# Two stores on two queues, merged waits and an earlier bias product in the tail of an attention and Mish decode kernel

## The chip, the cores and the metric

The kernel runs on one core of a Trainium2 chip. The metric is the device time of one execution in microseconds (us), and lower is better. The kernel before takes 669.4 us. Within one job its executions spread over 0.5 to 0.7 us.

## The reference, cut to what matters

```python
def reference(A_x, A_k_cache, A_v_cache, A_wq, A_wo, B_x, B_w1, B_b1, B_w2):
    # attention over a cache: 4 sequences, 32 heads, 4096 positions, head size 128
    h = x + attention(layernorm(x), k_cache, v_cache, wq) @ wo       # 4 x 640
    # feed-forward: 640 -> 1728 -> 640, Mish activation
    g = layernorm(h) @ w1 + b1
    act = g * tanh(softplus(g))
    return h + act @ w2                                              # 4 x 640, bf16
```

The two caches, read once, are 268 MB; all weights together are under 15 MB. What the change touches comes after the last cache tile: output projection, second layer norm, feed-forward and the store of 4 x 640 numbers.

## The kernel before

Some words first. SBUF is the memory in which the engines' tiles lie; its rows are called partitions. An engine *issues* a DMA, a transfer between memories; the DMA has *landed* when the last update of its semaphore (a counter that engines wait on) is seen. Of the two operands of a matmul, the *stationary* one is loaded into the array of TensorE first (LDWEIGHTS in a trace), and the *moving* one then passes through it (MATMUL). The *cast* below turns the result into bf16 before it is stored.

The kernel is written engine by engine. A small class keeps the semaphores: `need` waits for named results and `do` issues an instruction that may announce one. TensorE's main loop is a hardware loop, so some semaphores are counted back down by whoever waits on them (they are "taken"). Such a wait is an instruction of its own:

```python
            if sem in self.take:
                self.log.append((sem, d))
                if self.live:
                    self.eng.wait_ge(h, d).then_inc(h, -d)   # a separate instruction
            elif self.live:
                self.eng.wait_ge(h, n)                       # can ride on the next instruction
```

The tail of TensorE's program, cut:

```python
        wo_mm(2)
        wo_mm(3)                                   # each waits for its piece of wo
        ...                                        # sums for the layer norm
        pe.need("cen")
        for c0, c1 in zip(W1S, W1S[1:]):           # two pieces of w1
            pe.need(("w1", c0))
            if c1 == DC:
                pe.need("b1s")
                mm(red[:, 2, 0 : FC * N], ident_f[:, :], b1s[...], False, False)   # bias product
            for j in [FM] + list(range(FM)):       # the odd 64 features first, then 13 x 128
                ...                                # w1 products
        pe.need("h_lo")
        ...                                        # h (two bf16 parts) added to the result
        pe.need("act")
        def w2_mm(j):
            rows = P if j < FM else FT             # 128, or 64 for the odd features
            for k in range(CG):                    # four column groups of 160 outputs
                mm(y2_ps[k * QD : k * QD + N, :], act[0:rows, j, :], w2_..., ...)
        pe.need("w2t")
        w2_mm(FM)
        for j0, j1 in zip(W2S, W2S[1:]):           # three pieces of w2
            pe.need(("w2", j0))
            ...
```

The four column groups of the array compute 160 of the 640 outputs each. The four result rows of group k land in partitions 32k to 32k+3, and SyncE stores each group by itself:

```python
        sp.need("o_bf")
        for q in range(CG):
            load(sp, out_rows[:, q * OC : (q + 1) * OC], o_bf[q * QD : q * QD + N, :], ("out", q), "OUT")
        sp.need(("out", CG - 1))
```

The softmax here doesn't subtract the row's maximum and nothing guards it: scores larger than these inputs give would overflow.

Of the kernel before, what the change touches and what calls it, by code (L numbers as in the profile page):

```python
# [8 lines left out]
BF16 = mybir.dt.bfloat16  # L9
ACT = mybir.ActivationFunctionType  # L10
ALU = mybir.AluOpType
# [3 lines left out]
class Prog:  # L15
# [7 lines left out]
    def restart(self, live):  # L23
        self.live = live
        self.seen = {}
        self.count = {}
        self.log = []

    def need(self, *keys):
        if not self.book.ready:  # L30
            return
        want = {}
        for k in keys:
            sem, n = self.book.marks[k]
            if n > self.seen.get(sem, 0):
                want[sem] = max(n, want.get(sem, 0))
        for sem, n in want.items():
            d = n - self.seen.get(sem, 0)
            self.seen[sem] = n
            h = self.book.handles[sem]  # L40
            if sem in self.take:
                self.log.append((sem, d))
                if self.live:
                    self.eng.wait_ge(h, d).then_inc(h, -d)  # L44
            elif self.live:
                self.eng.wait_ge(h, n)

    def do(self, fn, mark=None, sem=None, by=1):
        ins = fn() if self.live else None
# [17 lines left out]
def kernel(  # L67
# [15 lines left out]
    N, _, D = A_x.shape  # L83
    _, H, Sk, Dh = A_k_cache.shape
    F = B_w1.shape[1]
    P = 128
# [14 lines left out]
    CG = 4  # L101
# [9 lines left out]

    book = Book()
    WSEM = ["WQ", "WT"] + [f"W{k}" for k in range(9)]
    for s in ["PE", "DV", "DVP", "DVA", "AC", "ACP", "PO", "KA", "KB", "VA", "VC", "X", "S", "OUT"] + WSEM:
        book.handles[s] = tc.alloc_semaphore(s)

    SB0, SLOT0 = 16512, 229344 - 3 * SLOT * 2
# [2 lines left out]
    def sb(name, shape, dt, region=at, top=SLOT0):  # L120
        size = 4 if dt == FP32 else 2
        for d in shape[1:]:
            size *= d
        size = -(-size // 32) * 32
        t = nc.alloc_sbuf_tensor_at(name, shape, dt, offset=region[0]).ap()
        region[0] += size
        assert region[0] <= top, (name, region[0])
        return t
# [61 lines left out]
    std2 = sb("std2", (P, N), FP32, tail, topA)  # L190
    rstd = sb("rstd", (P, N), FP32, tail, topA)
    b1s = sb("b1s", (P, FC, N), FP32, tail, topA)
    h_hi = sb("h_hi", (P, DC, N), BF16, tail, topA)
    h_lo = sb("h_lo", (P, DC, N), BF16, tail, topA)
    h1 = sb("h1", (P, FC, N), FP32, tail, topA)
    ta = sb("ta", (P, FC, N), FP32, tail, topA)
    tb = sb("tb", (P, FC, N), FP32, tail, topA)
    tb2 = sb("tb2", (P, FC, N), FP32, tail, topA)
    tb3 = sb("tb3", (P, FC, N), FP32, tail, topA)
    hm2 = sb("hm2", (P, FC, N), FP32, tail, topA)  # L200
    act = sb("act", (P, FC, N), BF16, tail, topA)
    o_bf = sb("o_bf", (P, OC), BF16, tail, topA)

    red = nc.alloc_psum_tensor("red", (P, 4, 512), FP32).ap()
# [32 lines left out]

    def load(p, dst, src, key, sem):
        p.do(lambda: p.eng.dma_start(out=dst, in_=src), key, sem, 16)

    def sync_prog():
        load(sp, slot["C"][:, 0 : DC * H * Dh], A_wq.rearrange("(p c) n -> p (c n)", c=DC), "wq", "WQ")

        def k_load(i):
            s = KS[i % N]
            load(sp, slot[s][:, :], tiles(A_k_cache, i), ("K", i), "K" + s)

        def v_load(i):
            s = VS[i % N]
            load(sp, slot[s][:, :], tiles(A_v_cache, i), ("V", i), "V" + s)  # L250

        for hg in range(NHG):
            i = hg * N
            if hg:
                sp.need(("PV", i - 2))
            k_load(i)
            if hg:
                sp.need(("F", i - 1, NS - 1))
            k_load(i + 1)
            sp.need(("PV", i - 1) if hg else ("qb", NHG - 1))  # L260
            v_load(i)
            sp.need(("F", i, NS - 1))
            k_load(i + 2)
            sp.need(("PV", i))
            v_load(i + 1)
            sp.need(("F", i + 1, NS - 1))
            k_load(i + 3)
            sp.need(("F", i + 2, NS - 1))
            v_load(i + 2)
            sp.need(("PV", i + 1))  # L270
            v_load(i + 3)
        sp.need(("F", NT - 1, NS - 1))
        for q in range(NHG):
            load(
                sp, wo_sb[:, q, :, :],
                A_wo[q * QN : (q + 1) * QN, :].rearrange("(p j) n -> p j n", j=G), ("wo", q), f"W{q}",
            )
        w1_v = B_w1.rearrange("(p c) n -> p c n", c=DC)
        for k, (c0, c1) in enumerate(zip(W1S, W1S[1:])):
            load(sp, w1_sb[:, c0:c1, :], w1_v[:, c0:c1, :], ("w1", c0), f"W{NHG + k}")  # L280
        sp.need(("PV", NT - 2))
        load(sp, w2_tail[0:FT, :], B_w2[FM * P : F, :], "w2t", "WT")
        w2_v = B_w2[0 : FM * P, :].rearrange("(p j) n -> p j n", j=FM)
        for k, (j0, j1) in enumerate(zip(W2S, W2S[1:])):
            load(sp, w2_sb[:, j0:j1, :], w2_v[:, j0:j1, :], ("w2", j0), f"W{NHG + 2 + k}")
        sp.need("o_bf")
        for q in range(CG):
            load(
                sp, out_rows[:, q * OC : (q + 1) * OC], o_bf[q * QD : q * QD + N, :],
                ("out", q), "OUT",  # L290
            )
        sp.need(("out", CG - 1))

    def pool_prog():
        g = nc.gpsimd
        po.do(lambda: g.memset(ident[:, :], 0.0), "id0", "PO")
        po.need("id0")
        po.do(
            lambda: g.affine_select(
                out=ident[:, :], in_=ident[:, :], compare_op=ALU.not_equal, fill=1.0, base=0,  # L300
                pattern=[[-1, P]], channel_multiplier=1,
            ),
            "ident", "PO",
        )
        po.do(lambda: g.memset(b1T[:, :], 0.0), "b1z", "PO")
        po.do(lambda: g.memset(lnT[:, :, :], 0.0), "lnz", "PO")
        po.do(lambda: g.memset(sel[:, :, :], 0.0), "selz", "PO")
        po.do(lambda: g.memset(selo[:, :, :], 0.0), "seloz", "PO")
        po.do(lambda: g.memset(ones[:, :], 1.0), "ones", "PO")
        po.need(("PV", NT - 2))  # L310
        po.do(lambda: g.memset(ones_d[:, :], 1.0 / D), "ones_d", "PO")
        po.do(lambda: g.memset(zeros[:, :], 0.0), "zeros", "PO")
        po.do(lambda: g.tensor_copy(out=ident_f[:, :], in_=ident[:, :]), "ident_f", "PO")

    def act_prog():
# [48 lines left out]
        for i in range(NT):  # L364
# [17 lines left out]
            lambda: a.activation(out=ta[:, :, :], in_=h1[:, :, :], func=ACT.Exp, scale=1.0),  # L382
            "ta", "AC",
        )

    def dve_prog():
        v = nc.vector
# [182 lines left out]
        for k in range(2):  # L570
# [8 lines left out]
            if k == 0:  # L579
# [18 lines left out]
            ),  # L598
            "var", DV,
        )  # L600
        dv.do(lambda: v.tensor_copy(out=h_hi[:, :, :], in_=st[:, 0, :, :]), "h_hi", DV)
        dv.need("std2", "b1b")
        dv.do(
            lambda: v.tensor_tensor(
# [6 lines left out]
        dv.need("h_hi")  # L611
        dv.do(
            lambda: v.tensor_tensor(
                out=h_lo[:, :, :], in0=st[:, 0, :, :], in1=h_hi[:, :, :], op=ALU.subtract
            ),
            "h_lo", DVP,
        )
# [26 lines left out]
        dv.need("tb3")  # L644
        dv.do(
            lambda: v.scalar_tensor_tensor(
                out=act[:, :, :], in0=tb3[:, :, :], scalar=-0.5, in1=hm2[:, :, :],
                op0=ALU.add, op1=ALU.mult,
            ),
            "act", DVP,  # L650
# [143 lines left out]
    def pe_tail():  # L794
# [6 lines left out]
                    mm(y_ps[:, c, :], w, a_t[:, k, j, :], False, done, "y" if done else None)  # L801

        hg = NHG - 1
        wo_mm(0)
        o_mm(NT - 1)
        l_mm(hg)
# [14 lines left out]
            )  # L821
        pe.need("cen")
        for c0, c1 in zip(W1S, W1S[1:]):
            pe.need(("w1", c0))
            if c1 == DC:
                pe.need("b1s")
                mm(
                    red[:, 2, 0 : FC * N], ident_f[:, :], b1s[:, :, :].rearrange("p j n -> p (j n)"),
                    False, False,
                )  # L830
            for j in [FM] + list(range(FM)):
                for c in range(c0, c1):
                    if j < FM:
                        w = w1_sb[:, c, 0 : FM * P].rearrange("p (f j) -> p j f", j=FM)[:, j, :]
                    else:
                        w = w1_sb[:, c, FM * P : F]
                    done = c == DC - 1 and j == FM - 1
                    mm(
                        h1_ps[0 : (P if j < FM else FT), j, :], w, cen[:, c, :], False, done,
                        "h1_ps" if done else None,  # L840
                    )
        pe.need("h_lo")
        for part in (h_hi, h_lo):
            for k in range(CG):
                for c in range(DC):
                    mm(
                        y2_ps[k * QD : k * QD + N, :].rearrange("b (m c) -> b c m", c=DC)[:, c, :],
                        part[:, c, :], ident[:, k * QD : (k + 1) * QD], False, False,
                    )
        pe.need("act")  # L850

        def w2_mm(j):
            rows = P if j < FM else FT
            for k in range(CG):
                cs = slice(k * OC, (k + 1) * OC)
                done = j == FM - 1 and k == CG - 1
                mm(
                    y2_ps[k * QD : k * QD + N, :], act[0:rows, j, :],
                    w2_sb[:, j, cs] if j < FM else w2_tail[0:FT, cs], False, j == FM - 1,
                    "y2" if done else None,  # L860
                )
# [67 lines left out]
```

## Time and profile before

| | before |
|---|---|
| time, median | 669.44 us |
| span in the trace | 667.4 us |
| last value tile lands | 637.1 us |
| first piece of w1 lands / first w1 matmul | 653.66 / 654.00 us |
| activation written / first w2 matmul | 660.91 / 661.21 us |
| first store issued / last store landed | 663.79 / 666.00 us |

Three lines of the page of the kernel before: the clock granted to TensorE and the share of busy DMA engines, both in tenths for 40 equal slices of the span, and the bytes read.

```profile
PEclk9668787879759796869557887878766878788875
DMA  9999999999999999999999999999999999999995
...
HBM read 283.35 MB, written 0.01 MB: 425 GB/s over the span
```

The DMA engines are busy for nine tenths or more of each slice but the last (one is 16.7 us). This reads as a kernel bound by memory until then, so that a change which moves the same bytes has its room in the tail. In the last slice TensorE runs at half its clock.

The timeline of the tail of the kernel before: start and length in us, engine, line, operation, output <- input, shapes, count; in brackets, idle time before it and what ended it.

```profile
637.21 5.27 PE L657 MATMUL pv<-slotC,e 128*32 128x512 bf16 x64 [11.19 <-PEq L44]
...
650.66 1.73 PE L657 MATMUL y_ps<-a_t,slotB 128*128 128x4 bf16 x40 [1.15 <-PEq L44]
...
653.53 0.18 DVE L582 TENSOR_TENSOR cen<-st,mu 128x20 bf16<-128x20 f32 x1
...
654.00 2.73 PE L657 MATMUL red<-cen,slotB 128*64 128x4 bf16 x42 [0.30 <-PEq L44]
...
656.59 0.66 PE L657 MATMUL red<-b1s,ident_f 128*128 128x56 f32 x2
...
657.18 1.93 PE L657 MATMUL red<-cen,slotB 128*64 128x4 bf16 x28
...
660.69 0.22 DVE L646 SCALAR_TENSOR_TENSOR act<-tb,hm 128x56 bf16<-128x56 f32 x1
...
661.21 0.30 PE L657 MATMUL red<-w_tail,act 64*4 64x160 bf16 x4 [1.35 <-PEq L44]
...
661.44 1.96 PE L657 MATMUL red<-slotA,act 128*4 128x160 bf16 x52
663.44 0.32 DVE L653 CAST o_bf<-red 128x160 bf16<-128x160 f32 x1 [2.53 <-PE red L657]
663.79 1.33 SPq L239 DMA_DIRECT2D out_dram<-o_bf  x4
```

It reads as a chain. The last wo stage starts at 650.66 because the last piece of wo landed at 650.37. The first piece of w1 lands at 653.66, and the first w1 matmul starts at 654.00. The bias product follows that stage directly at 656.59. VectorE writes the activation until 660.91, and w2 starts 0.30 us later. The cast ends at 663.76; four stores follow.

The waits of TensorE in the tail of the kernel before: waiter <- what ended the wait, total us, times, longest.

```profile
PE pv L657 <- PEq L44: 11.2, 1, 11.2
PE red L657 <- PEq L44: 1.6, 2, 1.3
PE y_ps L657 <- PEq L44: 1.1, 1, 1.1
```

"PEq" is TensorE's own sequencer. What ended the wait is the separate wait instruction of line 44, which ran after the result had arrived. At the first w1 stage and at w2 two of them stand in a row ahead of the first matmul (653.75 and 653.90, 660.95 and 661.10), each 0.05 us long. This is what the merging aims at.

The waits of SyncE at the end of the kernel before, same columns:

```profile
SPq L239 <- DMA out_dram<-o_bf: 0.9, 1, 0.9
```

Only 0.9 us pass between the end of the fourth issue and its landing. The rest of the 2.21 us from first issue to last landing is the issuing of the four stores one after another.

### The profile page before, as it was taken

The page shows a single profiled execution, that of the slowest core. Times are in us where ns is not written, and L with a number is a line of the kernel's source. Part 1 is how long each engine was busy: PE and PEld are TensorE (multiplying, and loading weights), DVE is VectorE, ACT ScalarE, POOL GpSimd, SP SyncE. Part 2 cuts the span into 40 slices and gives each one's busy share as a digit, 9 for nine tenths or more (in the row PEclk, how much of TensorE's full clock was granted, in tenths as well). Part 3 has the DMA queues.
Part 4 walks back from the last instruction along what each step waited for, and adds up shares of the span by engine and source line. Part 5 has one row for each costly group of instructions (what it writes and reads, how often), then busy time and mean ns, then how long its engine had stood idle before and what let it go on. Part 6 is the DMA issues. An engine that isn't in the chain of part 4 may idle for free. (4 is left out here: it accounts for less than half of the span.)

```text
span 667.4 us, 5166 instructions
## 1 busy us (share of the span) xinstructions
PE 394.1 (59%) x2729; PEld 79.4 (12%) x1769; DVE 406.5 (61%) x250; ACT 41.0 (6%) x157; POOL 2.6 (0%) x14
## 2 busy tenths in 40 slices
PE   0855748456327585847308395848426575847576
PEld 0700100101101010101100010100110010010155
DVE  1068988295058788666128798768208798849412
ACT  0200000000000010000000000000000000000011
POOL 1000000000000000000000000000000000000000
PEclk9668787879759796869557887878766878788875
DMA  9999999999999999999999999999999999999995
GB/s 378 437 440 440 433 420 409 441 440 437 429 436 436 436 436 424 424 440 436 432 432 440 436 432 432 416 440 436 433 432 436 440 436 433 428 425 440 428 396 198
DMA packets 6405, 283.55 MB, mean 425 GB/s; under 512 B 948, under 2 KB 1016, under 8 KB 1528
## 3 DMA queue, kind: packets, MB, share of 16 engines
q1 hardware_dynamic: 6160, 283.35, 98.5%
q8 instruction: 10, 0.16, 0.1%
q10 hardware_dynamic: 232, 0.01, 0.0%
q14 instruction: 3, 0.02, 0.0%
HBM read 283.35 MB, written 0.01 MB: 425 GB/s over the span
## 5 line engine op out<-in xcount | busy, mean ns | idle before, releaser
L466 DVE TENSOR_TENSOR slotA<-slotA,q_bc 128x8192 bf16<-128x8192 bf16 x32 | 140.7, 4416 | 110.9 <-DMA slotA<-in_A_k_cache_dram 110.7
L466 DVE TENSOR_TENSOR slotB<-slotB,q_bc 128x8192 bf16<-128x8192 bf16 x32 | 140.7, 4416 | 16.3 <-DMA slotB<-in_A_k_cache_dram 16.3
L667 PE MATMUL red<-slotA,ident 128*128 128x512 bf16 x480 | 141.0, 459 | 0.0
L477 DVE TENSOR_REDUCE s_f<-red 128x64 f32<-128x1024 f32 x64 | 78.1, 1220 | 96.9 <-PE red L667 96.8
L667 PE MATMUL red<-slotB,ident 128*128 128x512 bf16 x480 | 123.3, 415 | 0.0
L657 PE MATMUL red<-slotA,ident 128*128 128x512 bf16 x32 | 14.2, 445 | 119.3 <-PEq L44 119.3
L657 PE MATMUL pv<-slotC,e 128*32 128x512 bf16 x768 | 52.4, 434 | 42.7 <-PEq L44 42.7
L657 PE MATMUL red<-slotB,ident 128*128 128x512 bf16 x32 | 14.1, 441 | 87.0 <-PEq L44 87.0
L348 ACT ACTIVATE ex<-s_f 128x64 bf16<-128x64 f32 x64 | 16.4, 256 | 502.3 <-DVE s_f L477 502.3
L491 DVE TENSOR_TENSOR e<-ex,hmask 128x512 bf16<-128x512 bf16 x64 | 39.8, 682 | 0.0
L657 PEld LDWEIGHTS pv<-slotC,e 128*32 128x32 bf16 x768 | 22.5, 108 | 103.0 <-issue 89.4
L657 PEld LDWEIGHTS red<-slotA,ident 128*128 128x128 bf16 x32 | 3.2, 98 | 200.7 <-issue 200.6
L657 PEld LDWEIGHTS red<-slotB,ident 128*128 128x128 bf16 x32 | 3.2, 98 | 165.1 <-issue 165.1
L657 PEld LDWEIGHTS o_ps<-pv_sb,selo 128*32 128x32 f32 x128 | 12.7, 109 | 59.1 <-issue 59.1
L657 PE MATMUL o_ps<-pv_sb,selo 128*32 128x128 f32 x128 | 17.0, 276 | 0.0
L657 PE MATMUL pv<-slotA,e 128*32 128x512 bf16 x256 | 14.5, 380 | 0.9 <-PEq L44 0.9
L358 ACT COPY pv_sb<-pv 128x512 f32<-128x512 f32 x16 | 9.4, 585 | 75.7 <-PE pv L657 75.7
L348 ACT ACTIVATION_READ_ACCUMULATOR ex<-s_f 128x1 f32 x64 | 11.9, 186 | 0.0
L657 PE MATMUL red<-q_all,sel 32*128 32x128 bf16 x128 | 10.8, 280 | 0.8 <-PEq L44 0.8
L657 PEld LDWEIGHTS red<-q_all,sel 32*128 32x128 bf16 x128 | 10.6, 128 | 1.2 <-issue 1.2
L516 DVE RECIPROCAL rl<-misc 32x1 f32<-32x1 f32 x4 | 0.6, 150 | 16.2 <-PE misc L657 16.2
L657 PEld LDWEIGHTS pv<-slotA,e 128*32 128x32 bf16 x256 | 7.0, 97 | 22.1 <-issue 16.5
(93 smaller groups left out, 74.0 us busy)
## 6 DMA issues: line engine op xcount, KB each, us to landing
slotC<-in_A_wq_dram SPq DMA_DIRECT2D x1, 5120.0 KB, 15.1
slotB<-in_A_wo_dram SPq DMA_DIRECT2D x4, 1280.0 KB, 19.1
slotB<-in_B_w_dram SPq DMA_DIRECT2D x1, 1296.0 KB, 26.8
slotA<-in_B_w_dram SPq DMA_DIRECT2D x1, 960.0 KB, 30.3
slotB<-in_B_w_dram SPq DMA_DIRECT2D x1, 864.0 KB, 28.8
slotA<-in_B_w_dram SPq DMA_DIRECT2D x1, 800.0 KB, 32.0
slotA<-in_B_w_dram SPq DMA_DIRECT2D x1, 320.0 KB, 30.2
slotC<-in_A_v_cache_dram SPq DMA_DIRECT2D x12, 44.9
```

The source lines that it names most:

```text
L348: lambda: a.activation(out=ex[:, sl], in_=s_f[:, sl], func=ACT.Exp, scale=SCALE, accum_out=rs[:, b, s : s + 1],),
L358: lambda: a.copy(out=pv_sb[:, :, :].rearrange("p r d -> p (r d)"), in_=pv[:, :]),
L466: lambda: v.tensor_tensor(out=t, in0=t, in1=q_bc[:, hg, b, :].unsqueeze(1).to_broadcast([P, RS, Dh]), op=ALU.mult,),
L477: lambda: v.tensor_reduce(out=s_f[:, s * RS : (s + 1) * RS], in_=red[:, k : k + 2, :].rearrange("p k (r c) -> p (k r) c", c=CW), axis=AX.X ...
L491: lambda: v.tensor_tensor(out=e[:, sl, :], in0=ex[:, sl].unsqueeze(2).to_broadcast([P, RS, G]), in1=hmask[:, :].unsqueeze(1).to_broadcast( ...
L516: dv.do(lambda: v.reciprocal(out=rl[:, :], in_=l_ps), ("rl", hg), DV)
L657: lambda: nc.tensor.matmul(out_, lhsT=lhsT, rhs=rhs, start=start, stop=stop, skip_group_check=skip),
L667: return t.add_instruction(mybir.InstMatmult(name=nc.get_next_instruction_name(), engine=mybir.EngineType.PE, ins=[t.lower_ap(rhs), t.lowe ...
```

## The change

Its intent: two stores issued at once by two engines in place of four in a row; waits of TensorE after the loop carried by the instruction that needs the result, where it can; the bias product ahead of the wait for the second piece of w1. To cover two column groups with one store, the rows of the result must have one step throughout. So the operands `h_hi`, `h_lo` and `act` get 32 columns per group, of which every eighth is real and the rest is zero; the result rows then lie eight partitions apart. Cut to its core:

```diff
-            if sem in self.take:
+            if sem in self.take and self.base is None:      # freeze() before the tail sets base
...
             elif self.live:
-                self.eng.wait_ge(h, n)
+                low = self.base.get(sem, 0) if sem in self.take else 0
+                self.eng.wait_ge(h, n - low)
...
-    h_hi = sb("h_hi", (P, DC, N), BF16, tail, topA)
-    h_lo = sb("h_lo", (P, DC, N), BF16, tail, topA)
-    act = sb("act", (P, FC, N), BF16, tail, topA)
+    ROW = QD // N                                            # 8
+    spread = sb("spread", (P, 2 * DC + FC, N, ROW), BF16, tail, topA)   # zeroed by GpSimd
+    h_hi, h_lo, act = (slices of spread)
...
+    def store(p, h):
+        c, n = CG // 2, D // 2
+        p.need("o_bf")
+        load(
+            p, out_rows[:, h * n : (h + 1) * n].rearrange("b (k o) -> k b o", k=c),
+            o_bf[h * P // 2 : (h + 1) * P // 2 : ROW, :], ("out", h), f"OUT{h}",
+        )
...
+        store(sp, 0)           # SyncE
+        store(ac, 1)           # ScalarE
...
-                out=act[:, :, :], in0=tb3[:, :, :], scalar=-0.5, in1=hm2[:, :, :],
+                out=act[:, :, :, 0], in0=tb3[:, :, :], scalar=-0.5, in1=hm2[:, :, :],
...
-            pe.need(("w1", c0))
             if c1 == DC:
                 pe.need("b1s")
                 mm(...)                                      # bias product
+            pe.need(("w1", c0))
...
-                    y2_ps[k * QD : k * QD + N, :], act[0:rows, j, :],
+                    y2_ps[k * QD : (k + 1) * QD, :],
+                    act[0:rows, j, :, :].rearrange("p n r -> p (n r)"),
```

More of the change, by code (lines that the diff above doesn't have):

```diff
@@ L27, in restart, with freeze @@
         self.log = []
+        self.base = None
+    def freeze(self):
+        self.base = dict(self.seen)
     def need(self, *keys):
@@ L113 @@
     WSEM = ["WQ", "WT"] + [f"W{k}" for k in range(9)]
-    for s in ["PE", "DV", "DVP", "DVA", "AC", "ACP", "PO", "KA", "KB", "VA", "VC", "X", "S", "OUT"] + WSEM:
+    for s in ["PE", "DV", "DVP", "DVA", "AC", "ACP", "PO", "KA", "KB", "VA", "VC", "X", "S", "OUT0", "OUT1"] + WSEM:
         book.handles[s] = tc.alloc_semaphore(s)
@@ L192 @@
     b1s = sb("b1s", (P, FC, N), FP32, tail, topA)
-    h_hi = sb("h_hi", (P, DC, N), BF16, tail, topA)
-    h_lo = sb("h_lo", (P, DC, N), BF16, tail, topA)
+    ROW = QD // N
+    spread = sb("spread", (P, 2 * DC + FC, N, ROW), BF16, tail, topA)
+    h_hi, h_lo, act = (
+        spread[:, j0:j1, :, :] for j0, j1 in ((0, DC), (DC, 2 * DC), (2 * DC, 2 * DC + FC))
+    )
     h1 = sb("h1", (P, FC, N), FP32, tail, topA)
@@ L239, in load @@
         p.do(lambda: p.eng.dma_start(out=dst, in_=src), key, sem, 16)
+    def store(p, h):
[4 more added lines that the diff above has]
+            o_bf[h * P // 2 : (h + 1) * P // 2 : ROW, :], ("out", h), f"OUT{h}",
+        )
     def sync_prog():
@@ L285, in sync_prog @@
             load(sp, w2_sb[:, j0:j1, :], w2_v[:, j0:j1, :], ("w2", j0), f"W{NHG + 2 + k}")
-        sp.need("o_bf")
-        for q in range(CG):
-            load(
-                sp, out_rows[:, q * OC : (q + 1) * OC], o_bf[q * QD : q * QD + N, :],
-                ("out", q), "OUT",
-            )
-        sp.need(("out", CG - 1))
+        store(sp, 0)
+        sp.need(("out", 0), ("out", 1))
     def pool_prog():
@@ L311, in pool_prog @@
         po.do(lambda: g.memset(ones_d[:, :], 1.0 / D), "ones_d", "PO")
+        po.do(lambda: g.memset(spread[:, :, :, :], 0.0), "spread", "PO")
         po.do(lambda: g.memset(zeros[:, :], 0.0), "zeros", "PO")
@@ L600, in dve_prog @@
         )
-        dv.do(lambda: v.tensor_copy(out=h_hi[:, :, :], in_=st[:, 0, :, :]), "h_hi", DV)
+        dv.do(lambda: v.tensor_copy(out=h_hi[:, :, :, 0], in_=st[:, 0, :, :]), "h_hi", DV)
         dv.need("std2", "b1b")
@@ L613, in dve_prog @@
             lambda: v.tensor_tensor(
-                out=h_lo[:, :, :], in0=st[:, 0, :, :], in1=h_hi[:, :, :], op=ALU.subtract
+                out=h_lo[:, :, :, 0], in0=st[:, 0, :, :], in1=h_hi[:, :, :, 0], op=ALU.subtract
             ),
@@ L803, in pe_tail @@
         hg = NHG - 1
+        pe.freeze()
         wo_mm(0)
@@ L846, in pe_tail @@
                     mm(
-                        y2_ps[k * QD : k * QD + N, :].rearrange("b (m c) -> b c m", c=DC)[:, c, :],
-                        part[:, c, :], ident[:, k * QD : (k + 1) * QD], False, False,
+                        y2_ps[k * QD : (k + 1) * QD, :].rearrange("b (m c) -> b c m", c=DC)[:, c, :],
+                        part[:, c, :, :].rearrange("p n r -> p (n r)"), ident[:, k * QD : (k + 1) * QD], False, False,
                     )
```

## The prediction

> **What bounds the kernel now.** The page's slices show the DMA engines at 9 tenths in every slice but the last (425 GB/s over 667.4 us), while PE is busy 59% and VectorE 61%. The cache stream is untouched. The last value tile lands at 637.1 us; from there the change acts. In the timeline of the tail, weights still stream until 661.9 us and pace TensorE twice: the last wo piece lands at 650.37 (fourth wo stage starts 650.63), the first w1 piece at 653.66 (first w1 stage starts 653.97). Then compute is the limit: w1 stages to 659.1, VectorE and ScalarE chain to 660.91, w2 661.18 to 663.4, cast to 663.76, four stores issued one after another by SyncE, 663.79 to 665.12, the last landing at 666.0, and 1.4 us of fixed program end.
>
> **What the change does, costed.**
>
> 1. Stores. Issues follow each other by 0.31 to 0.39 us; each store lands about 1.18 us after its own issue began; first issue to last landing is 2.21 us. Two stores issued together leave one latency, perhaps 1.2 to 1.4 us: eight rows each, and ScalarE's issue can be slower (its three early issues took 0.39 to 0.92 us). Gain 0.8 to 1.0 us, all critical. The Trainium skill, "DMA: Bandwidth & Descriptors", section "Issuing engines are not separate DMA queues", says issuing from several engines saves only sequencer issue time; that is exactly this term.
>
> 2. Waits. TensorE's standalone consuming waits come 0.15 us apart, and a matmul follows the last by about 0.08. After the activation ends (660.91) w2 starts 0.27 us later behind two of them; a wait carried by the instruction itself (statistics after the copy, 652.61 to 652.66) costs 0.05. Each matmul carries one wait; of a pair, the other stays separate, but ahead, where it has long been met. I expect 0.2 us at the first w1 stage, 0.2 at w2, and 0.1 in w2's stream (bubble after its first four matmuls). The fourth wo stage also starts 0.2 earlier, but w1's landing swallows that.
>
> 3. Bias product ahead of the wait. The second w1 piece has landed by 656.1, while the first stage runs to 656.55; the bias product follows without a gap. Gain 0.
>
> 4. Stationary operands of 32 columns, not 4, for the h and w2 products. w2's matmuls run in rounds of four at 0.133 us, 160 columns at the granted clock of 0.5, so moving data is the limit, and weight loads should hide, as in the value products (64 in 5.27 us). I allow 0.05 us, at risk up to 1 us if the column groups' loads serialize; the Trainium skill, "TensorEngine Tiling (Array Packing)", "Key Properties", says tiles load and multiply in parallel. The h products sit inside the activation chain (1.0 us of slack).
>
> 5. The added zeroing on GpSimd, near 622, is waited for only 20 us later: 0.
>
> Sum: 0.9 + 0.5 - 0.05, about 1.35 us.
>
> **Prediction: 668.1 us, 667.4 to 669.0; faster by over 2% 0.5%, within 2% 99%, slower 0.5%.**
>
> **What would show it.** Last value landing near 637; first w1 stage about 0.1 us after its piece's landing; activation end to first w2 matmul 0.05 to 0.1 us; w2 stage 2.0 to 2.2 us (2.3 now); one store on each queue, both landed within 1.4 us after the cast; bias product directly behind the first w1 stage, before and after.
>
> **What would make it wrong.** ScalarE's store late (issue over 0.6 us, or contention for descriptor generation); 32-column loads pacing w2; weights landing later by chance: 0.2 us of DMA jitter is as large as any wait term.

## The result, and the profile after

The changed kernel takes 668.78 us (668.64 to 668.85, 4 runs) and the kernel before 669.43 us (669.37 to 669.85). The ratio is 0.9989, 95% interval 0.9971 to 1.0006. A ratio is the mean time of one kernel's runs over that of the other's in the same rounds, so it is not quite the ratio of the medians quoted. The interval includes 1, although each of the four runs of the changed kernel is faster than every run of the other here; by a margin of 2% the two count as the same. A later job (e10 below) gave 668.79 against 669.35 us. The medians put the gain at about 0.6 us where 1.35 was predicted. Traces show where the rest went.

From the page of the changed kernel:

```profile
PEclk9658787879759796869668687968766878788975
DMA  9999999999999999999999999999999999999995
...
HBM read 283.35 MB, written 0.01 MB: 425 GB/s over the span
```

Memory is as full as before, and the bytes are the same. The timeline of the tail of the changed kernel:

```profile
637.15 5.38 PE L670 MATMUL pv<-slotC,e 128*32 128x512 bf16 x64 [11.18 <-PEq L49]
...
650.49 1.76 PE L670 MATMUL y_ps<-a_t,slotB 128*128 128x4 bf16 x40 [0.98 <-DMA slotB<-in_A_wo_dram]
...
653.38 0.18 DVE L595 TENSOR_TENSOR cen<-st,mu 128x20 bf16<-128x20 f32 x1
...
653.87 2.71 PE L670 MATMUL red<-cen,slotB 128*64 128x4 bf16 x42 [0.31 <-DMA slotB<-in_B_w_dram]
...
656.44 0.65 PE L670 MATMUL red<-b1s,ident_f 128*128 128x56 f32 x2
...
657.02 1.92 PE L670 MATMUL red<-cen,slotB 128*64 128x4 bf16 x28
...
660.52 0.41 DVE L659 SCALAR_TENSOR_TENSOR spread<-tb,hm 128x56 bf16<-128x56 f32 x1
...
660.99 0.32 PE L670 MATMUL red<-w_tail,spread 64*32 64x160 bf16 x4 [1.24 <-DVE spread L659]
...
661.24 1.92 PE L670 MATMUL red<-slotA,spread 128*32 128x160 bf16 x52
663.21 0.33 DVE L666 CAST o_bf<-red 128x160 bf16<-128x160 f32 x1 [2.28 <-PE red L670]
663.57 0.66 SPq L247 DMA_DIRECT2D out_dram<-o_bf  x1
663.57 0.64 ACTq L247 DMA_DIRECT2D out_dram<-o_bf  x1
```

The activation is written into `spread` and takes 0.41 us where it took 0.22. The matmuls follow 0.06 us after it, where they took 0.30. The two stores are issued together, but each issue takes 0.64 to 0.66 us; an issue took 0.27 to 0.35 before.

The waits of TensorE in the tail of the changed kernel:

```profile
PE pv L670 <- PEq L49: 11.2, 1, 11.2
PE red L670 <- DVE spread L659: 1.2, 1, 1.2
PE y_ps L670 <- DMA slotB<-in_A_wo_dram: 1.0, 1, 1.0
PE red L670 <- DMA slotB<-in_B_w_dram: 0.3, 1, 0.3
```

The profile now puts the end of each wait down to the result itself (an instruction of VectorE or a DMA). Between 640 and 664 us TensorE has 6 separate wait instructions left, where it had 22. One of them still stands ahead of the first w1 stage, for the piece of w1 (653.76 to 653.81, after its landing at 653.73); the wait for `cen` is carried by the weight load behind it. The first line is the product of the last value tile; it lies before the tail and its wait is still separate.

The wait of SyncE for the stores in the changed kernel:

```profile
SPq L52 <- DMA out_dram<-o_bf: 1.3, 1, 1.3
```

From the end of its own issue SyncE now waits 1.3 us, where it waited 0.9. It waits for ScalarE's store; its own has landed 1.69 us after the first issue, ScalarE's after 1.96.

All of the difference, from the records of the two traces. The landing is when the last update of a DMA's semaphore is seen. "Again" is the second trace of the changed kernel.

| stretch of the chain | before, us | changed, us | again, us | change (first trace) | predicted |
|---|---|---|---|---|---|
| first piece of w1 lands, at | 653.66 | 653.73 | 653.58 | +0.07 | chance |
| to first w1 matmul | 0.34 | 0.14 | 0.14 | -0.21 | -0.2 |
| to activation written | 6.90 | 7.06 | 7.08 | +0.16 | 0 |
| to first w2 matmul | 0.30 | 0.06 | 0.06 | -0.25 | -0.2 |
| to start of the cast | 2.23 | 2.23 | 2.23 | 0.00 | -0.05 |
| to first store issued | 0.35 | 0.35 | 0.35 | 0.00 | 0 |
| first issue to last landing | 2.21 | 1.96 | 1.95 | -0.25 | -0.8 to -1.0 |
| to end of span | 1.44 | 1.48 | 1.48 | +0.05 | 0 |

Before rounding, the changes of the first trace add up to -0.42 us, which is the difference of the two spans (667.44 to 667.01). Chance in the landing of weights hides 0.07 of it. In the kernel before, `cen` came 0.04 us after the piece of w1, and from there the first matmul took 0.30 us. So 0.16 of the 0.21 us were earned at this wait, and 0.04 because `cen`, behind a merged wait at the last wo stage, was no longer the later of the two. Two terms are off: the stores earned 0.25 us and not 0.9, and writing the activation costs 0.19 us that the prediction did not list.

### The profile page after: what moved, and what is told of

Its sections match the earlier page's. It is cut to its first block, busy times and chain, and to the rows that moved or that the text cites. A ratio compares the mean times of both kernels' runs of the same rounds, so it can differ in the third digit from the quotient of the medians.

```text
span 667.0 us, 5150 instructions
## 1 busy us (share of the span) xinstructions
PE 393.0 (59%) x2729; PEld 79.2 (12%) x1769; DVE 406.8 (61%) x250; ACT 41.1 (6%) x157; POOL 3.3 (0%) x15
## 5 line engine op out<-in xcount | busy, mean ns | idle before, releaser
L680 PE MATMUL red<-slotA,ident 128*128 128x512 bf16 x480 | 137.9, 451 | 0.0
L680 PE MATMUL red<-slotB,ident 128*128 128x512 bf16 x480 | 126.0, 421 | 0.0
L670 PE MATMUL red<-slotA,ident 128*128 128x512 bf16 x32 | 14.4, 451 | 120.1 <-PEq L49 120.1
L670 PE MATMUL red<-slotB,ident 128*128 128x512 bf16 x32 | 14.2, 445 | 89.4 <-PEq L49 89.4
```

The costliest lines, as they stand in the source:

```text
L670: lambda: nc.tensor.matmul(out_, lhsT=lhsT, rhs=rhs, start=start, stop=stop, skip_group_check=skip),
L680: return t.add_instruction(mybir.InstMatmult(name=nc.get_next_instruction_name(), engine=mybir.EngineType.PE, ins=[t.lower_ap(rhs), t.lowe ...
```

## The experiments

Kernels of one job ran on the same chip; there were three jobs of four kernels (e1 to e4, e6 to e9, and e10, e5, e11, e12). All twelve are within 2% of the kernel before, so what follows rests on traces more than on times. First came four that ask about the stores and the waits. Theory A was that two issues at the same time share one generator of descriptors (the orders that a DMA is made of). Theory B was that the eight-row store itself is slow.

### Four serial stores in the changed kernel (e1_four_serial)

```diff
-        store(sp, 0); sp.need(("out", 0), ("out", 1))      # and store(ac, 1)
+        for q in range(4): load(sp, out_rows[:, q * OC : (q + 1) * OC],
+                                o_bf[q * QD : (q + 1) * QD : ROW, :], ("out", q), "OUT0")
```

> The changed kernel with its store part alone undone: four stores of four rows, all issued by SyncE, as before (they now read rows at a step of eight partitions). Changed kernel: first issue to last landing 1.96 us (663.57 to 665.53), each issue 0.64 to 0.66 us. Both theories of the stores (A: two issues at the same time share one generator of descriptors; B: an eight-row store with a two-level row pattern takes longer to issue and to start, whoever issues it) expect here what before showed: issues of 0.27 to 0.35 us, first issue to last landing 2.2 us, so 0.25 us more than the changed kernel, about 669.0 us. It gives what the store part really earned. The strided write of the activation should still take 0.41 us.

670.42 us (before 669.35 us, ratio 1.0016, 1.0002 to 1.0029): slower than either kernel. From the timeline of this kernel:

```profile
660.44 0.41 DVE L658 SCALAR_TENSOR_TENSOR spread<-tb,hm 128x56 bf16<-128x56 f32 x1
...
663.48 2.62 SPq L247 DMA_DIRECT2D out_dram<-o_bf  x4
```

The four issues together take 2.62 us; before, the same count took 1.33. Singly they take 0.58 to 0.73 us, and 3.68 us pass from first issue to last landing. Nothing was issued at the same time, and each store has four rows as before. Neither theory expected this: something slows an issue that both left out. Among the stores only the step between the rows in SBUF differs from before. With serial stores of stepped rows as the starting point, two eight-row stores on two queues are worth 1.7 us (3.68 to 1.96), but the layout made for them takes 1.5 of that first.

### Two eight-row stores, both by SyncE (e2_two_serial)

```diff
-        store(ac, 1)                # ScalarE
+        store(sp, 1)                # SyncE, after store(sp, 0)
```

> The changed kernel with both eight-row stores issued by SyncE, one after the other, ScalarE issuing none. Theory A (sharing between two simultaneous issues): each issue back at 0.3 to 0.35 us, first landing 1.2 us after its issue, all landed 1.55 us after the first issue, 0.4 us faster than the changed kernel. Theory B (the eight-row pattern itself is slow): each issue stays 0.5 to 0.66 us, the first lands about 1.7 us after its issue and the second about 2.3, so 0.3 us slower than the changed kernel, about 669.1.

669.17 us. From its timeline, the two issues together:

```profile
663.53 1.23 SPq L247 DMA_DIRECT2D out_dram<-o_bf  x2
```

Singly they take 0.66 and 0.52 us; the first store lands 1.69 us after its issue and the second at 2.29 us, all as theory B had it. Issues stay slow with no second engine at work, so simultaneous issue is not what made them slow. The second queue is worth 0.33 us here.

### Four-row stores of stepped rows on two queues (e3_four_two_queues)

```diff
-        store(sp, 0)                # and store(ac, 1)
+        store(sp, (0, 1))           # and store(ac, (2, 3)): one column group each,
+                                    # o_bf[q * QD : (q + 1) * QD : ROW, :]
```

> The changed kernel with four-row stores, two issued by SyncE and two by ScalarE. Theory A (simultaneous issues share): issues stretch to 0.6 us or so on both queues, and all have landed 2.0 to 2.3 us after the first issue, no gain over the changed kernel. Theory B (eight-row pattern slow, queues independent): issues 0.3 us each, all landed 1.5 us after the first issue, 0.45 us faster than the changed kernel, about 668.3.

669.53 us; issues 0.60 to 0.73 us; 2.75 us to the last landing. It is worse than what either theory gave, and it fits with e1 in one thing: every issue of stepped rows is slow, and each queue has two of them. But in e1 the second store had landed 2.43 us after the first issue. With another queue at work it takes 0.33 us more, so in this form the queues do hold each other up after the issue; how, no run shows.

### The merged waits alone (e4_waits_only)

```diff
 # kernel before, plus only:
+        pe.freeze()                 # and the two lines of need() as in the change
         wo_mm(0)
```

> The kernel before with the merged waits alone: bias order, narrow stationary operands, contiguous activation and four serial stores as before. Theory: the merged waits earn 0.2 us before the first w1 stage less whatever the landing of w1 takes back, and 0.22 us between the activation and w2; activation write 0.22 us (not 0.41). So the cast of the result starts 0.35 to 0.4 us before that of the kernel before (663.44), near 663.05, and the time is about 669.05. The rival, that merging moved only waiting time with nothing earned, expects 669.43. The gap after w2's first four matmuls (0.25 us between first weight loads in both kernels) stays if it comes from the change from 64 to 128 rows of the array; it falls to about 0.13 if the separate wait made it.

668.90 us against 669.35 us (ratio 0.9990, 0.9977 to 1.0004). From its timeline:

```profile
660.84 0.22 DVE L651 SCALAR_TENSOR_TENSOR act<-tb,hm 128x56 bf16<-128x56 f32 x1
...
661.11 0.30 PE L662 MATMUL red<-w_tail,act 64*4 64x160 bf16 x4 [1.10 <-DVE act L651]
```

In its trace the w1 piece happened to land late, at 654.02, so stretches are compared. From landing to first w1 matmul 0.14 us (before 0.34); activation written (0.22 us, at 661.05) to first w2 matmul 0.05 (before 0.30); w2 to the cast 2.19 (before 2.23). From landing to cast it is 9.28 us where before took 9.78: the merged waits earn 0.5 us in this pair of traces, the sum that was predicted. The expected place of the cast (663.05) was missed only by the late landing; it started at 663.30. The pause after w2's first four matmuls stayed at 0.23 us, so waits do not cause it.

Theory C, formed now: reading rows at a step of partitions makes a store slow to issue, and two queues do work side by side. Three of the next four kernels test it; the fourth (e9) asks about the pause.

### Dense rows and two queues (e6_two_queues_dense)

```diff
 # e4, with
-        four stores on SyncE
+        store(sp, (0, 1))           # o_bf[q * QD : q * QD + N, :], adjacent rows
+        store(ac, (2, 3))
```

> Merged waits with the layout of before (narrow stationary operands, result rows in four adjacent partitions per column group, activation written densely) and the four stores split two to SyncE and two to ScalarE. Theory C, formed from the four serial stores of stepped rows (issues of 0.58 to 0.73 us against 0.27 to 0.35): reading result rows at a step of partitions is what makes a store slow to issue, and two queues do work side by side. It expects issues of 0.27 to 0.4 us here, first issue to last landing 1.5 us (2.2 with one queue), so 0.7 us less than the merged waits alone: about 668.2 us, 0.55 us better than the changed kernel. Theory A (simultaneous issues share one generator) expects issues of 0.6 us and 2.1 us to the last landing, no gain over the merged waits alone, 668.9.

668.29 us (before 669.25, ratio 0.9986, 0.9973 to 1.0000). From its timeline:

```profile
660.47 0.22 DVE L655 SCALAR_TENSOR_TENSOR act<-tb,hm 128x56 bf16<-128x56 f32 x1
...
663.27 0.66 SPq L244 DMA_DIRECT2D out_dram<-o_bf  x2
663.28 0.66 ACTq L244 DMA_DIRECT2D out_dram<-o_bf  x2
```

Two issues on each queue together take 0.66 us, as long as one issue in the changed kernel. Singly they take 0.27 to 0.35 us, on ScalarE as on SyncE, and at the same time. The last landing comes 1.74 us after the first issue, 0.47 us less than before. 1.5 was expected, and SyncE's second store kept to it (1.56 us); ScalarE's landed 0.19 us after that, though its packets left only 0.03 us later. Theory A, a longer issue, is out for stores of this form.

### A step of two partitions (e7_step_two)

```diff
 # e1, with
-    ROW = QD // N                   # 8
+    ROW = 2                         # operands 8 columns wide
```

> The changed kernel with four serial four-row stores, but the rows two partitions apart in place of eight (stationary operands 8 columns wide, every second one zero). If any step above one makes the issue slow: issues near 0.6 us, first issue to last landing 3.6 us, about 670.4. If the slowness grows with the step, issues near 0.35 us and 2.3 us in all, about 669.0. The activation's write at a step of two elements: 0.41 us if any step slows it, nearer 0.22 if it goes by the distance of 16 bytes.

670.26 us. From its timeline:

```profile
660.74 0.22 DVE L658 SCALAR_TENSOR_TENSOR spread<-tb,hm 128x56 bf16<-128x56 f32 x1
...
663.55 2.63 SPq L247 DMA_DIRECT2D out_dram<-o_bf  x4
```

Issues take 0.58 to 0.73 us, and 3.67 us pass to the last landing, as with a step of eight. Of the two steps tried, two and eight, both made the issue equally slow. The activation's write took 0.22 us: there the distance does matter. A distance of four bytes from element to element cost nothing that can be seen, sixteen cost 0.19 us; where between them the cost begins, no run shows.

### Wide operands with adjacent rows (e8_wide_dense)

```diff
 # e1, with
-    spread = sb("spread", (P, 2 * DC + FC, N, ROW), ...)
+    spread = sb("spread", (P, 2 * DC + FC, ROW, N), ...)   # the four real columns first
```

> Stationary operands of 32 columns as in the changed kernel, but with the four real columns side by side (28 zero columns after them), so the result rows lie in adjacent partitions as before; four serial stores. Theory: width costs nothing and the step costs all. Activation write 0.22 us rather than 0.41, w2 from first to last matmul start 1.80 us as with narrow operands, store issues 0.27 to 0.35 us and 2.2 us to the last landing: as the merged waits alone, 668.9 us within 0.15. Rival, that the width of the operands or the buffer that GpSimd zeroes costs something: activation write still 0.41 us, or w2 slower than 1.85 us, and 669.1 or more.

668.83 us. From its timeline:

```profile
660.42 0.22 DVE L658 SCALAR_TENSOR_TENSOR spread<-tb,hm 128x56 bf16<-128x56 f32 x1
...
663.27 1.34 SPq L247 DMA_DIRECT2D out_dram<-o_bf  x4
```

The same 32 columns, the same zeroing by GpSimd; the activation is back at 0.22 us and four issues at 1.34 us in all. The width costs little: w2 from first matmul to cast takes 2.23 us where narrow operands took 2.19 (e4, e6); from its first to its last matmul start it is 1.84 us, and 1.80 was expected. The strides cost the rest.

### The odd 64 features padded to 128 (e9_full_tail)

```diff
 # e6, with
-    w = w1_sb[:, c, FM * P : F]                 # 64 columns
+    w = w1_sb[:, c, F - P : F]                  # 128 columns, 64 of them again
-    rows = P if j < FM else FT
+    rows = P                                    # the first 64 rows of the w2 tail zeroed by GpSimd
```

> Kernel of two dense queues with the 64 odd features of the feed-forward part padded to whole 128-row, 128-column work: the w1 tail takes the last 128 columns of w1 (64 of them a second time), and the matching upper rows of the w2 tail are zero. The arithmetic result is the same. Theory: the pause after the tail's matmuls (0.125 us instead of 0.06 between starts in both w1 stages, 0.23 us instead of 0.13 after w2's first four) comes from the change between a 64-wide and a 128-wide tile of the array, not from waits. Padded: w2's first round to second 0.13 us, no 0.125 us gap in the w1 stages, 0.2 us in all, about 668.0 us. Rival: the pause is a start-up cost of the stage, and stays; then the same time as two dense queues.

668.01 us, against 668.29 for e6 in the same job (ratio to before 0.9983, 0.9969 to 0.9996). From its timeline:

```profile
660.47 0.30 PE L667 MATMUL red<-w_tail,act 128*4 128x160 bf16 x4 [1.10 <-DVE act L656]
660.56 1.95 PE L667 MATMUL red<-slotA,act 128*4 128x160 bf16 x52
```

Between the starts of w2's first and second round 0.09 us pass, not 0.23; the gap of 0.125 us in each w1 stage is gone. The trace of e9 is 0.37 us shorter than that of e6, more than the 0.2 expected, because the tail's own matmuls in w1 also follow faster (starts 0.03 us apart, not 0.05). The Trainium skill, "TensorEngine Tiling (Array Packing)", "Key Properties", says that changing the tiling mode drains TensorE; these traces agree with that, though they do not show the drain as such; that a 64-wide tile loads or multiplies more slowly by itself is not ruled out.

### The changed kernel again (e10_after_again)

No edit.

> The changed kernel itself again, unaltered, on the chip of the runs sent with it, for a fair comparison: 668.8 us within 0.3, first issue to last landing of its stores 1.96 us, activation write 0.41 us.

668.79 us; 1.95 us to the last landing; activation written in 0.41 us.

### The bias product alone (e5_bias_only)

```diff
 # kernel before, with
-            pe.need(("w1", c0))
             if c1 == DC: ...         # bias product
+            pe.need(("w1", c0))
```

> The kernel before with the bias product alone put ahead of the wait for the second piece of w1. Prediction's reading: that piece has landed (656.09) before the first stage's matmuls end (656.55), so nothing waits and nothing is earned: time as before within 0.1 us or so of its run-to-run spread, first matmul of the first stage to last matmul of the second 4.90 us as before. Rival: the separate wait held up the queue behind it, so that the stage shortens by 0.1 us or more.

669.51 us against 669.35 us (ratio 1.0001). From the first matmul of the first w1 stage to the last start of the second 4.89 us pass, where before has 4.90. It earns nothing in this kernel, as predicted.

### Eight adjacent rows, a wrong result (e11_eight_dense_wrong)

```diff
-            o_bf[h * P // 2 : (h + 1) * P // 2 : ROW, :]
+            o_bf[h * P // 2 : h * P // 2 + c * N, :]     # rows 0..7, not the right ones
```

> Wrong result on purpose: the changed kernel, whose two eight-row stores read eight adjacent rows of the result buffer in place of every eighth row. It measures the store term of the prediction by itself. If the step between the rows is the whole cause, issues come back to 0.35 us and both stores have landed 1.3 to 1.5 us after the first issue (the prediction's 1.2 to 1.4), 0.5 to 0.65 us faster than the changed kernel run with it, about 668.2 us. If eight rows over two groups on few DMA engines also cost, issues stay over 0.5 us and 1.9 us in all.

The result is wrong, as meant (relative error 0.93). 668.85 us, no faster than the changed kernel. From its timeline:

```profile
663.42 0.76 SPq L247 DMA_DIRECT2D out_dram<-o_bf  x1
663.42 0.75 ACTq L247 DMA_DIRECT2D out_dram<-o_bf  x1
```

Issues take 0.76 and 0.75 us with adjacent rows, and 2.06 us pass to the last landing. So the step is not the whole cause, and theory C in its plain form falls too: an eight-row store is slow with adjacent rows as well, which is what theory B said. Put together:

| store | rows adjacent: one issue, us | rows stepped: one issue, us |
|---|---|---|
| 4 rows, one group | 0.27 to 0.35 (before, e4, e6, e8) | 0.58 to 0.73 (e1, e3, e7) |
| 8 rows, two groups (destination nested in two levels) | 0.75 to 0.76 (e11) | 0.52 to 0.66 (changed, again, e2) |

Only one of the four forms is fast, and the two departures do not add up. Which of the two things in the second row of the table matters, eight rows or the nested destination, no run tells apart. A third thing goes with them: the Trainium skill, "DMA: Bandwidth & Descriptors", "Why a DMA increments its semaphore by 16 and not by 1", says that each DMA engine used by a DMA of SyncE or ScalarE updates its semaphore once, and that the issuing sequencer adds the rest. A four-row store left five updates in the trace and an eight-row store three, so the one ran on four DMA engines and the other on two. None of the runs shows what the issuing engine does in the added 0.3 to 0.4 us.

### The best version (e12_best_bias)

```diff
 # e9, plus the bias product ahead of the wait, as in e5
```

> The best kernel so far (merged waits, dense rows, two queues, full-width tail) with the bias product ahead of the wait as well. Its first w1 stage ends at about the moment when the second w1 piece lands, so the order may now matter by up to 0.1 us: 667.9 to 668.0 us, and 0.8 us or so faster than the changed kernel run with it.

667.84 us (before 669.35 us, ratio 0.9979, 0.9965 to 0.9992), 0.95 us faster than the changed kernel in the same job. Its timeline at the end:

```profile
660.12 0.22 DVE L656 SCALAR_TENSOR_TENSOR act<-tb,hm 128x56 bf16<-128x56 f32 x1
...
660.39 0.30 PE L667 MATMUL red<-w_tail,act 128*4 128x160 bf16 x4 [1.10 <-DVE act L656]
...
660.47 1.95 PE L667 MATMUL red<-slotA,act 128*4 128x160 bf16 x52
...
662.83 0.66 SPq L244 DMA_DIRECT2D out_dram<-o_bf  x2
662.83 0.66 ACTq L244 DMA_DIRECT2D out_dram<-o_bf  x2
```

Here the bias order does something. In e9 the second piece of w1 landed at 656.30 and the bias product started at 656.35, behind its wait; in e12 it started at 656.26 and the piece landed at 656.29. From the first w1 matmul to the bias product 2.46 us pass, in e9 2.55 (one trace of each, from different chips).

## Why the prediction was right or wrong

The time lay within the predicted range (667.4 to 669.0), 0.2 us under its top. The range was 1.6 us wide and reached down to a gain of 0.4, so this says little. Each of the three parts of the change acted in the direction predicted, but the sum was not right: 1.35 us predicted, about 0.6 measured.

- **Term 1, the stores, was mis-sized.** The prediction put it so: "Two stores issued together leave one latency, perhaps 1.2 to 1.4 us ... Gain 0.8 to 1.0 us, all critical." It measured 1.96 us and a gain of 0.25. The step took the latency of a store of four adjacent rows (about 1.18 us from its issue to its landing) as that of any small store. The new form takes 0.64 to 0.66 us to issue. Its first packet also leaves 1.25 us after the start of the issue on SyncE and 1.53 on ScalarE; a store of before needs 0.77. The form of the store makes the issue slow, not two engines issuing: SyncE alone had the same slow issues (e1, e2), and two engines with the old form were quick (e6). So the form explains the landing of SyncE's store at 1.69 us, which e2 repeats with nothing beside it. The last 0.27 us, to 1.96, is not explained by it: ScalarE's packets leave 0.28 us after those of SyncE, though issued together, in e11 as well, but only 0.03 us after them in e6. That the queues hold each other up with the slow forms, as in e3, would fit; no run shows it. The prediction named "issue over 0.6 us" among the risks, but for ScalarE alone, and it did not widen the term.
- **A term was missing.** VectorE's write of the activation became strided, 56 elements of bf16 each 16 bytes from the last, and went from 0.217 to 0.406 us on the critical path. The strided write itself is shown as the cause: the same data at four bytes' distance took 0.223 us (e7), and with four adjacent elements per group 0.216 us (e8). The Trainium skill, "SBUF — State Buffer", in "Door 1: The DMA port swizzle", describes 16-byte lines and a penalty for each access that crosses to a new one. The case agrees on the distance: with 16 bytes every element is on another line.
- **Term 2, the waits, was right in sum, in part by luck.** 0.21 and 0.25 us were saved at the two places, as read from the chain (e4 shows the same without the rest). Of the 0.1 us put on the pause in w2's stream, about 0.04 came with narrow operands (2.23 to 2.19 us). The pause of 0.23 us, for which the prediction put the 0.1 us, is not a wait's; it goes when the tail has the full width (e9). The Trainium skill, "Perfetto Trace Analysis", "Identifying Dependency Chains", says that separate semaphore instructions may be inserted ahead of an instruction that waits on several engines; here they were also there for single waits that count down, 0.05 us long and 0.15 us apart.
- **Term 3, the bias order, was right at zero** (e5), and worth up to 0.09 us once the rest is faster (e12).
- **Term 4, the wide operands, was right**: 0.04 us against the 0.05 allowed, and the loads of 32 columns hid behind rounds of 0.133 us. That moving data is the limit there agrees with the value products: at the same clock of 0.5 a round of 512 columns took 0.427 us, 3.2 times as long for 3.2 times the columns. **Term 5**, the zeroing by GpSimd (0.74 us at 621.6), cost nothing that a trace shows.

So 0.9 + 0.5 - 0.05 became, by the table of stretches, 0.25 for the stores, 0.46 for the waits at the two places, 0.00 for w2's stream (0.04 earned, 0.04 paid for width), less 0.16 before the activation's end and less 0.05 for one more wait of SyncE at the end: 0.50 us in all.

## What to carry to other kernels

Count what a rearrangement costs the engines that must write and issue it, not only the instructions it saves: here a layout made so that one store could do the work of two about doubled the time of each issue and of the vector write before it, and two queues with the old simple stores did better. Before pricing a DMA by another one's issue time, look for one of the same form in a trace: the same number of rows, the same step, the same nesting. In this tail, where each result releases the next, two separate wait instructions in a row cost 0.16 and 0.25 us more than merged ones at the two places where they came last, so merging them was worth doing.

## What the Trainium skill lacked or had wrong

- "DMA: Bandwidth & Descriptors", "Anatomy of one DMA", calls descriptor generation "small, variable" for the path of GpSimd, and "Issuing engines are not separate DMA queues" calls the sequencer's issue time usually small next to the DMA. Neither says that it depends on the form of a small store: 0.27 to 0.35 us for four adjacent rows of 320 bytes, 0.58 to 0.73 for the same rows at a step of two or eight partitions, 0.75 to 0.76 for eight adjacent rows to a nested destination, 0.52 to 0.66 for eight stepped ones. In a store of 5 KB in all, issuing is over half of the time (1.33 of 2.21 us before).
- "SBUF — State Buffer" gives no size for the penalty of a strided write, and the table of strides in "Vector Engine (DVE) Microarchitecture Reference", "Measured stream behaviour on trn2", is for 4-byte words and not for bf16: here 0.19 us for 56 bf16 elements at 16 bytes (3.4 ns each), nothing seen at 4 bytes.
- "TensorEngine Tiling (Array Packing)", "Key Properties", gives no time for the drain between tiling modes: w2's second round started 0.23 us after its first with a change from 64 to 128 rows, 0.09 us without one, both at half the clock.
